# Attention on one core: three score banks and four maxima banks, weighted values in halves, the accumulator out as two tiles, the last pairs with wide exponentials

## The chip, the core and the metric

The kernel runs on one core of a Trainium2 chip. The metric is the time of one execution on the device in microseconds (us). Engines are named as in the profile: PE (TensorE matmul) and PEld (its weight loads), DVE (VectorE), ACT (ScalarE), POOL (GpSimd) and SP (SyncE, which issues most transfers).

## The reference

A block of a transformer for 2048 rows of width 512: softmax attention with 32 heads of width 16, and behind it a gated mixer (gMLP). The change lies in attention and in what takes its output.

```python
h  = x + attention(layernorm(x), wqkv, wo)         # 32 heads, Dh = 16, S = 2048
p  = softmax(q @ k.T / 4)                          # per head, 2048 x 2048
o  = p @ v
h2 = h + mixer(layernorm(h), w_in, w_sp, b_sp, w_out)
```

All is computed in float32 accuracy: q and k as pairs of float16 parts stacked on the contraction rows, the weighted values in float32.

## The kernel before, in words

A first stage projects q, k and v and writes them to memory. Then comes attention, in one loop over 512 units (`hg`, `qb`, `kb`): 8 groups of four heads, 4 query blocks of 512 rows, 16 key blocks of 128 keys. The loop's body handles two units, a **pair**; eight pairs make one query block of a group, here called a block. All engines work in program order, so the order in which the body is written is the order on each engine.

What a pair holds:

- **Scores** (`score`, L778 to 788): eight matmuls `s<-qst,kst`, 128 keys by 512 queries, for two key blocks and four heads. Head index t picks the upper or lower half of the array's rows (rows 0 to 49 or 64 to 113). Each is followed by an exponential on ACT, `pt<-s` (L788). Their PSUM pool `ps_s` has four banks.
- **Maxima steps** (`max_pair`, L205 to 254): the row maxima which softmax subtracts are found eleven pairs ahead (`LEAD`), by eight small steps per pair. A step is a matmul `m<-...,qst` into a bank of `ps_m` (three banks, taken in turn), then a reduction on DVE (`mx<-m`, L228). Two of the steps go together: `minus` takes its bank by an `Abs` on ACT (`ab<-m`, L233), `plus` adds that to its own bank on DVE (L237). The step behind the eighth closes a block's maxima (`nm`, on DVE and POOL), and `max_rows` turns them and writes them into q's spare rows.
- **Weighted values** (`weigh`, L790 to 797): for one key block four float32 matmuls `pv<-pt,vst`, one per head, on four column groups of the array, into one PSUM bank (`ps_v`). Each appears as two records, so one `weigh` is eight records. A ones column in `vst` makes the sum of the exponentials appear as a 17th row of each head. The second key block's `weigh` of a pair is issued in the next pair.

The eighth PSUM bank is `ps_v`'s: 4 + 3 + 1. At a block's end `gather` (L800 to 811) copies the accumulator `pv` to one tile `og`, 256 columns on DVE (L803) and 256 on ACT (L804), and issues eight transfers: values to `o_scr`, sums to a small tile. Three pairs later `invert` takes reciprocals and writes them to `r_scr`.

POOL meanwhile splits and scales the mixer's weights (`work`). The last 11 pairs have no maxima steps. In them the first rows of the output projection start: `load_o` reads o and the reciprocals `rc`, POOL multiplies them (L726), `split_o` makes two float16 parts (L731, L732), `make_h` runs 12 matmuls with `wo` and adds x. Then the mixer's first stage makes all other rows of h in the same manner, one in a step, and later stages follow that the diff does not touch.

The order within a pair before, as the body writes it (s0 to s7 scores, M0 to M7 maxima steps as `max_pair` lists them, W and P the two `weigh`): s0 M0 M1 s1 s2 s3 M2 W M3 M4 s4 s5 s6 M5 turn s7 M6 M7 P, with M3 `minus` and M6 `plus`.

Of the kernel before, what the change touches and what calls it, by code (L numbers as in the profile page):

```python
# [38 lines left out]
VW = DH + 1  # L39
FB = [(i * P, min(P, FH - i * P)) for i in range(6)]  # L40
# [18 lines left out]
def block_kernel(ctx: ExitStack, tc: tile.TileContext, x, wqkv, wo, w_in, w_sp4, b_sp, w_out, out):  # L59
# [25 lines left out]
    o_scr = dram.tile([D, S], F32, name="o_scr")  # L85
# [119 lines left out]
    def max_pair(m):  # L205
# [33 lines left out]
        def last(b):  # L239
            one(1, 3, b)  # L240
# [13 lines left out]
        return [four[0], two[0], two[1], minus, four[1], four[2], plus, last]  # L254
# [15 lines left out]
    with ExitStack() as pre:  # L270
# [260 lines left out]
        todo, done = [], [0]  # L531

        def ahead(k):
            for _ in range(k):
                m = done[0] // 8
                if not todo and m < LEAD:
                    steps = max_pair(m)
                    todo.extend(steps[i] for i in (0, 1, 4, 2, 5, 3, 6, 7))
                if todo:
                    todo.pop(0)(done[0] % 5)  # L540
                    done[0] += 1

# [171 lines left out]
    def load_o(sb):  # L714

        c = slice(sb * P, (sb + 1) * P)
        o = e2.tile([P, DB, P], F32, name="o")
        nc.sync.dma_start(o, o_scr[:, c].rearrange("(d p) s -> p d s", p=P))
        rc = e2.tile([P, DB, P], F32, name="rc")
        for d in range(DB):  # L720
            nc.sync.dma_start(rc[:, d, :], r_scr[8 * d:8 * d + 8, c].rearrange(
                "h (o s) -> h o s", o=1).to_broadcast([8, DH, P]))
# [3 lines left out]
        return lambda: nc.gpsimd.tensor_mul(o, o, rc)  # L726
# [7 lines left out]
    def make_h(sb, acc):  # L734

        o2, h = o2s.pop(sb), xrs[sb]
        for d in range(DB):
            mm3(acc, o2[0][:, d, :], o2[1][:, d, :], wo2[0][:, d, :], wo2[1][:, d, :],
                d == 0, d == DB - 1)
# [17 lines left out]
    def invert():  # L757
# [4 lines left out]
        for j in range(4):  # L762
            nc.sync.dma_start(r_scr[head(hg, j % 2, j // 2), cols].rearrange("(p c) -> p c", c=16),
                              rc[32 * j:32 * j + 32, :])
# [3 lines left out]
    with ExitStack() as at:  # L768
# [9 lines left out]
        def score(hg, qb, kb, p, t):  # L778

            if not t:  # L780
                pts[p, kb] = pp.tile([P, 2, 512], F32, name="pt")
            turn[0] += 1
            pool = later[0] if later and turn[0] % 6 > 3 else ps_s
            s = pool.tile([P, 512], F32, name="s")
            r = slice(RG * t, RG * t + KM)
            nc.tensor.matmul(s, kst[hg % 2][r, p, kb * P:(kb + 1) * P],  # L786
                             qst[hg * NQ + qb][r, p, :], start=True, stop=True)
            nc.scalar.activation(pts[p, kb][:, t, :], s, AF.Exp, scale=scales_[hg // 2])  # L788

        def weigh(hg, qb, kb):  # L790
            if kb == 0:
                pv[0] = ps_v.tile([P, 512], F32, name="pv")
            for j in range(4):
                c = (4 * kb + j) * VW
                nc.tensor.matmul(pv[0][32 * j:32 * j + 32, :], vst[hg % 2][:, c:c + 32],  # L795
                                 pts[j % 2, kb][:, j // 2, :], start=kb == 0, stop=kb == NB - 1)
            for p in range(2):
                del pts[p, kb]

        def gather(hg, qb, pool=sm):  # L800

            o = pool.tile([P, 512], F32, name="og", bufs=2)
            nc.vector.tensor_copy(o[:, :256], pv[0][:, :256])  # L803
            nc.scalar.activation(o[:, 256:], pv[0][:, 256:], AF.Copy)  # L804
            cols = slice(qb * 512, (qb + 1) * 512)
            sums = pool.tile([P, 16], F32, name="sums")
            for j in range(4):
                h = head(hg, j % 2, j // 2)
                nc.sync.dma_start(o_scr[h * DH:(h + 1) * DH, cols], o[32 * j:32 * j + DH, :])
                nc.sync.dma_start(sums[32 * j:32 * j + 32, :], o[32 * j + DH:32 * j + VW, :])  # L810
# [210 lines left out]
        prev, turn, count, later, asked, pts = None, [0], [0], [], [], {}  # L1021
        for n in range(0, len(units), 2):
# [17 lines left out]
            if not steps and not later:  # L1040
                maxima.close()
                later.append(attn.enter_context(
                    tc.tile_pool(name="ps_l", bufs=2, space=PSUM, side="right")))

            def step():
                if steps:
                    steps.pop(0)(count[0] % 3)
                    count[0] += 1

            both = lambda k, p, *ts: [score(hg, qb, k, p, t) for t in ts]  # L1050
            both(kb, 0, 0)
            step()
            step()
            both(kb, 0, 1)
            both(kb, 1, 0, 1)
            step()
            if prev is None:

                pv[0] = ps_v.tile([P, 512], F32, name="pv")
                for j in range(4):  # L1060
                    nc.tensor.matmul(pv[0][32 * j:32 * j + 32, :], vst[0][:, :32],
                                     vst[0][:, :512], start=True, stop=True)
            else:
                weigh(*prev)
            if kb == 0 and n:
                gather(*units[n - 1][:2])
            step()
            step()
            both(kb1, 0, 0, 1)
            both(kb1, 1, 0)  # L1070
            step()
            if turned:
                max_rows()
            both(kb1, 1, 1)
            step()
            step()
            weigh(hg, qb, kb)
# [3 lines left out]
            if n in (486, 490, 506):  # L1081
                asked.append(load_o(h_rows[min((n - 486) // 4, 2)]))
            if n in (492, 496, 508):
                asked.pop(0)()
            if n in (494, 502):
                split_o(h_rows[(n - 494) // 8])
            if n in (500, 504):
                sb = h_rows[(n - 500) // 4]
                make_h(sb, later[0].tile([P, 512], F32, name="h", bufs=1))
# [5 lines left out]
        gather(*prev[:2], e2)  # L1095
# [20 lines left out]
    with ExitStack() as mid:  # L1116
# [67 lines left out]
        with tc.manual_schedule(engines={E.PE, E.Activation, E.DVE, E.Pool, E.SP}):  # L1184
# [3 lines left out]
            for k in range(NB):  # L1188
                sb, new = row[k], row.get(k + 2)
                if new is not None:  # L1190
                    make_h(new, ps.tile([P, 512], F32, name="acc"))
# [207 lines left out]
```

## Time and profile before

| | |
|---|---|
| time, median of 3 runs | 1768.5 us (1768.03 to 1769.24) |
| the profiled execution's own time | 1767.71 us |
| its span, first to last instruction | 1765.9 us |
| attention's pairs with maxima steps | 161.8 to 1275.4 us |
| the last 11 pairs | 1275.4 to 1324.9 us |
| mean granted clock of TensorE | 0.999 |

A row of the timeline gives start, length, engine, line, operation, output and inputs with their shapes, and a count where alike instructions in a row are merged; a bracket holds idle time of the engine ahead of it and what ended that. A row of the groups ends in busy time, mean ns of one, and idle time ahead of them. Since an engine takes up the next instruction before the last one has ended, lengths overlap, and the step from one to the next is shorter than the length of one. Busy time is the union of the lengths.

### The profile page before, as it was taken

How to read it: one execution, taken by the hardware profiler on the slowest of the kernel's cores; microseconds unless marked ns; L12 is line 12 of the kernel's file. 1: busy time of each engine (PE TensorE's matmuls, PEld its weight loads, DVE VectorE, ACT ScalarE, POOL GpSimd, SP SyncE). 2: the span in 40 equal slices, each digit the busy share in tenths (PEclk: the TensorE clock that was granted, in tenths of full speed). 3: DMA queues.
4: the chain of work that ended last, by engine and by line, in shares of the span. 5: the costliest groups of instructions: out<-in, count | busy, mean ns of one | idle time of the engine just before them, and what ended most of it. 6: DMA issues, size and time to landing. Idle time of an engine off the chain costs nothing.

```text
span 1765.9 us, 32751 instructions
## 1 busy us (share of the span) xinstructions
PE 1725.2 (98%) x11621; PEld 643.5 (36%) x11621; DVE 1395.1 (79%) x2896; ACT 1324.2 (75%) x2638; POOL 825.8 (47%) x1088
## 2 busy tenths in 40 slices
PE   9999999999999999999999999999999999999999
PEld 4433222222222222222222222222225666777776
DVE  7688999999999999999999999999825886111112
ACT  4335999999999999999999999999984554011000
POOL 1322677765772178776777667600002765100010
PEclk9999999999999999999999999999999999999999
DMA  5534332242220145335244434300023563753450
GB/s 179 159 101 141 88 84 84 80 91 69 79 58 22 55 122 147 116 115 143 87 147 109 129 113 136 89 16 5 23 64 106 141 178 121 270 186 130 155 182 24
DMA packets 188028, 191.71 MB, mean 109 GB/s; under 512 B 70568, under 2 KB 139240, under 8 KB 187864
## 3 DMA queue, kind: packets, MB, share of 16 engines
q1 hardware_dynamic: 185560, 183.99, 35.6%
q10 hardware_dynamic: 2304, 5.64, 0.8%
q8 instruction: 91, 1.49, 0.4%
q14 instruction: 73, 0.60, 0.1%
HBM read 124.66 MB, written 64.56 MB: 107 GB/s over the span
## 4 chain that ended last, share of the span: by engine, by line
PE 69%; DVE 14%; ACT 11%; DMA 2%; issue 2%; POOL 2%; SPq 1%; DVEq 0%; ACTq 0%; POOLq 0%
PE pv L795 20%; PE m L223 12%; PE s L786 11%; ACT pt L788 7%; DVE mx L228 7%; PE acc L107 4%; PE acc L109 4%; PE acc L108 4%; PE g L107 4%; PE g L108 4%; PE g L109 4%; ACT ab L233 2%; DVE ab L237 1%; DVE rs_t L124 1%; DVE rs_u L126 1%
## 5 line engine op out<-in xcount | busy, mean ns | idle before, releaser
L788 ACT ACTIVATE pt<-s 128x512 f32<-128x512 f32 x2048 | 1042.9, 620 | 7.9 <-PE s L786 5.0
L228 DVE TENSOR_REDUCE mx<-m 128x1 f32<-128x512 f32 x1510 | 963.6, 683 | 21.8 <-PE m L223 3.6
L795 PE MATMUL pv<-pt,vst 128*32 128x512 f32 x4096 | 555.1, 605 | 0.9 <-ACT og L804 0.9
L223 PE MATMUL m<-kst,qst 48*128 48x512 f16 x1510 | 527.6, 379 | 0.1
L786 PE MATMUL s<-qst,kst 50*128 50x512 f16 x2048 | 443.0, 377 | 0.4 <-DVE mx L228 0.4
L223 PEld LDWEIGHTS <-qst 48*128 48x128 f16 x2048 | 143.7, 93 | 389.0 <-issue 376.5
L786 PEld LDWEIGHTS <-kst 50*128 50x128 f16 x2048 | 125.4, 95 | 315.9 <-issue 229.3
L223 PE MATMUL m<-uvs,qst 48*128 48x512 f16 x504 | 190.4, 379 | 24.9 <-ACT ab L233 18.6
L246 POOL TENSOR_SCALAR nm<-nm 128x16 f32<-128x16 f32 x32 | 6.6, 206 | 389.3 <-DVE nm L243 368.8
L237 DVE CUSTOM_DVE_ANT_0 ab<-m,ab 128x512 f32<-128x512 f32 x252 | 171.0, 679 | 7.8 <-PE m L223 5.1
L233 ACT ACTIVATE ab<-m 128x512 f32<-128x512 f32 x252 | 151.8, 602 | 17.1 <-PE m L223 16.4
L795 PEld LDWEIGHTS pv<-pt,vst 128*32 128x32 f32 x4096 | 83.4, 108 | 179.7 <-issue 170.5
L1268 ACT ACTIVATE pT<-tp 128x384 fp32r<-128x384 f32 x32 | 14.0, 488 | 142.1 <-PE tp L1260 142.0
L1346 POOL TENSOR_TENSOR pr<-pr,z 128x344 f32<-128x344 f32 x8 | 7.3, 912 | 193.0 <-DVE pr L1345 181.6
L966 POOL TENSOR_TENSOR op<-raw,op 128x512 f16<-128x512 f32 x80 | 92.8, 1160 | 5.8
L873 POOL TENSOR_TENSOR raw<-raw 128x512 f32<-128x512 f32 (+1 forms) x84 | 83.2, 991 | 6.3
L878 POOL TENSOR_TENSOR acc_sp<-acc_sp,raw 128x512 f32<-128x512 f32 x63 | 80.4, 1277 | 4.4
L107 PE MATMUL acc<-wi,hT 128*128 128x344 f16 x256 | 79.1, 309 | 0.0
L108 PE MATMUL acc<-wi,hT 128*128 128x344 f16 x256 | 79.1, 309 | 0.0
L109 PE MATMUL acc<-wi,hT 128*128 128x344 f16 x256 | 79.1, 309 | 0.0
L1290 DVE TENSOR_TENSOR y<-acc,h 128x512 f32<-128x512 f32 x16 | 11.1, 692 | 85.6 <-PE acc L1286 84.2
L726 POOL TENSOR_TENSOR o<-o,rc 128x512 f32<-128x512 f32 x16 | 20.3, 1270 | 100.1 <-DMA rc<-r_scr 98.3
(233 smaller groups left out, 2297.1 us busy)
## 6 DMA issues: line engine op xcount, KB each, us to landing
raw<-in_w_sp SPq DMA_DIRECT2D x128, 256.0 KB
s_scr<-op SPq DMA_DIRECT2D x64, 256.0 KB
op<-s_scr SPq DMA_DIRECT2D x32, 512.0 KB
a_scr<-op SPq DMA_DIRECT2D x48, 256.0 KB
op<-a_scr SPq DMA_DIRECT2D x24, 512.0 KB
qst<-q_scr SPq DMA_DIRECT2D x192, 32.0 KB
kst<-k_scr SPq DMA_DIRECT2D x48, 128.0 KB
raw<-in_w_in SPq DMA_DIRECT2D x32, 172.0 KB
```

The lines of the kernel that those rows point to most:

```text
L107: nc.tensor.matmul(ps, lh, rh, start=first, stop=False, **kw)
L108: nc.tensor.matmul(ps, lh, rl, start=False, stop=False, **kw)
L109: nc.tensor.matmul(ps, ll, rh, start=False, stop=last, **kw)
L223: nc.tensor.matmul(acc, q[r, p, c], keys[r, p], start=True, stop=True)
L228: nc.vector.reduce_max(at(t, e if t else e - 1), acc, axis=AX.X)
L233: nc.scalar.activation(ab[0], acc, AF.Abs)
L237: nc.vector.tensor_tensor_reduce(ab[0], acc, ab[0], 0.5, LOW, ALU.add, ALU.max, at(0, 0))
L786: nc.tensor.matmul(s, kst[hg % 2][r, p, kb * P:(kb + 1) * P], qst[hg * NQ + qb][r, p, :], start=True, stop=True)
L788: nc.scalar.activation(pts[p, kb][:, t, :], s, AF.Exp, scale=scales_[hg // 2])
L795: nc.tensor.matmul(pv[0][32 * j:32 * j + 32, :], vst[hg % 2][:, c:c + 32], pts[j % 2, kb][:, j // 2, :], start=kb == 0, stop=kb == NB - 1)
L873: pool.tensor_mul(got[0] if n else acc, got[0], got[0])
L966: chores.append((lambda: pool.tensor_sub(t[0][:, 1], of(), t[0][:, 0]), TT))
```

## The change

1. PSUM: `ps_s` has three banks, and a fourth maxima bank `m3` is added, so that steps take four banks in turn.
2. The pair's order is written out in two tables, `PAIR`, and `PAIR0` for the first pair of a block. Scores and maxima steps alternate such that neighbours use different halves of the array's rows. `H` is half of the previous unit's weighted values: 256 of the 512 query columns.
3. The accumulator leaves as two tiles, `og1` (128 columns, ACT) and `og0` (384 columns, DVE), by four transfers into an `o_scr` of 32 rows per head; the sums are read back from there a pair later.
4. In the last 11 pairs two scores share a tile of two banks, and one exponential takes 1024 columns (`scores2`); `make_h` is a generator, whose matmuls come three to a pair.
5. `load_o` reads o by four transfers; `load_o`, its product and `split_o` stand some pairs earlier; `invert` writes by two transfers instead of four.

```diff
+PAIR = "s0 M0 s2 M4 M1 s1 H s3 M2 s5 M3 H M5 s4 M7 s6 turn s7 M6 P".split()
+PAIR0 = "M1 s1 M0 s0 M4 s2 H s3 s4 M5 H out1 M3 out0 s5 M2 M7 s6 turn s7 M6 P".split()
-    o_scr = dram.tile([D, S], F32, name="o_scr")
+    o_scr = dram.tile([DB, 8, 32, S], F32, name="o_scr")
...
-        nc.sync.dma_start(o, o_scr[:, c].rearrange("(d p) s -> p d s", p=P))
+        for d in range(DB):
+            nc.sync.dma_start(o[:, d, :], o_scr[d, :, :DH, c])
...
-        ps_s = at.enter_context(tc.tile_pool(name="ps_s", bufs=4, space=PSUM))
+        ps_m3 = inner.enter_context(tc.tile_pool(name="ps_m3", bufs=1, space=PSUM))
+        ps_s = inner.enter_context(tc.tile_pool(name="ps_s", bufs=3, space=PSUM))
+        more[3] = lambda: ps_m3.tile([P, 512], F32, name="m3")
...
+        def scores2(hg, qb, kb, p):
+            pts[p, kb] = pp.tile([P, 2, 512], F32, name="pt")
+            turn[0] += 1
+            s = later[turn[0] % 3 == 0].tile([P, 2, 512], F32, name="s2")
+            for t in range(2):
+                product(s[:, t, :], hg, qb, kb, p, t)
+            nc.scalar.activation(pts[p, kb], s, AF.Exp, scale=scales_[hg // 2])
-        def weigh(hg, qb, kb):
+        def weigh(hg, qb, kb, a=0, b=512):
...
-                nc.tensor.matmul(pv[0][32 * j:32 * j + 32, :], vst[hg % 2][:, c:c + 32],
-                                 pts[j % 2, kb][:, j // 2, :], start=kb == 0, stop=kb == NB - 1)
+                nc.tensor.matmul(pv[0][32 * j:32 * j + 32, a:b], vst[hg % 2][:, c:c + 32],
+                                 pts[j % 2, kb][:, j // 2, a:b], start=kb == 0, stop=kb == NB - 1,
+                                 skip_group_check=True)
...
-            o = pool.tile([P, 512], F32, name="og", bufs=2)
-            nc.vector.tensor_copy(o[:, :256], pv[0][:, :256])
-            nc.scalar.activation(o[:, 256:], pv[0][:, 256:], AF.Copy)
+            a, b = (0, OG) if i == 0 else (OG, 512)
+            ogs[i] = pool.tile([P, b - a], F32, name=f"og{i}", bufs=2)
+            if i:
+                nc.scalar.activation(ogs[i], pv[0][:, a:b], AF.Copy)
+            else:
+                nc.vector.tensor_copy(ogs[i], pv[0][:, a:b])
...
+            if not steps:
+                scores2(hg, qb, kb, 0)
+                scores2(hg, qb, kb, 1)
+                some_h(2)
+                weigh(*prev)
...
+                scores2(hg, qb, kb1, 0)
+                scores2(hg, qb, kb1, 1)
+                some_h(1)
+                weigh(hg, qb, kb)
...
-            if n in (486, 490, 506):
-                asked.append(load_o(h_rows[min((n - 486) // 4, 2)]))
+            if n in (476, 480, 506):
+                asked.append(load_o(h_rows[min((n - 476) // 4, 2)]))
```

PE's rows before, at the end of an ordinary pair (m0 to m2 are the maxima banks, `uvs` marks the products of `minus` and `plus`, s a score, pv the weighted values):

```order
L223 LDWEIGHTS qst_8807
L223 MATMUL m1_10203<-kst1_1855,qst_8807 128x512
L786 LDWEIGHTS kst1_1855
L786 MATMUL s_10206<-qst_8255,kst1_1855 128x512
L223 LDWEIGHTS qst_8807
L223 MATMUL m2_10209<-uvs1_1856,qst_8807 128x512
L223 LDWEIGHTS qst_8807
L223 MATMUL m0_10212<-kst1_1855,qst_8807 128x512
L795 MATMUL pv_9995<-pt_10158,vst1_163 32x512
L795 MATMUL pv_9995<-pt_10171,vst1_163 32x512
L795 MATMUL pv_9995<-pt_10158,vst1_163 32x512
L795 MATMUL pv_9995<-pt_10171,vst1_163 32x512
```

The `plus` product stands in bank m2, and so did `minus` of this pair, three steps earlier; then comes a whole weighted values. PE's rows now, at the same place:

```order
L226 LDWEIGHTS qst_9788
L226 MATMUL m2_11001<-kst0_164,qst_9788 128x512
L798 LDWEIGHTS kst1_1855
L798 MATMUL s_11005<-qst_9157,kst1_1855 128x512
L798 LDWEIGHTS kst1_1855
L798 MATMUL s_11008<-qst_9157,kst1_1855 128x512
L226 LDWEIGHTS qst_9788
L226 MATMUL m3_11011<-uvs0_165,qst_9788 128x512
L823 MATMUL pv_11014<-pt_10948,vst1_163 32x512
L823 MATMUL pv_11014<-pt_10961,vst1_163 32x512
L823 MATMUL pv_11014<-pt_10948,vst1_163 32x512
L823 MATMUL pv_11014<-pt_10961,vst1_163 32x512
```

`plus` has moved to bank m3, and every maxima product stands beside a score. In the middle of a pair PE now has:

```order
L798 LDWEIGHTS kst1_1855
L798 MATMUL s_10955<-qst_9157,kst1_1855 128x512
L226 LDWEIGHTS qst_9788
L226 MATMUL m2_10958<-kst0_164,qst_9788 128x512
L798 LDWEIGHTS kst1_1855
L798 MATMUL s_10962<-qst_9157,kst1_1855 128x512
L823 MATMUL pv_10403<-pt_10903,vst1_163 32x256
L823 MATMUL pv_10403<-pt_10924,vst1_163 32x256
L823 MATMUL pv_10403<-pt_10903,vst1_163 32x256
L823 MATMUL pv_10403<-pt_10924,vst1_163 32x256
L798 LDWEIGHTS kst1_1855
L798 MATMUL s_10969<-qst_9157,kst1_1855 128x512
```

The weighted values of the previous unit have become two pieces of 256 columns, of which this is the first, with scores and steps between them. DVE's rows at a block's turn before, with what each waits for:

```order
L228 TENSOR_REDUCE mx<-m_12871 128x1 [waits PE_49]
L228 TENSOR_REDUCE mx<-m_12884 128x1 [waits PE_49]
L803 COPY og<-pv 128x256 [waits PE_49]
L228 TENSOR_REDUCE mx<-m_12907 128x1 [waits PE_49]
L228 TENSOR_REDUCE mx<-m_12921 128x1 [waits PE_49]
```

and now:

```order
L231 TENSOR_REDUCE mx<-m_13430 128x1 [waits PE_49]
L231 TENSOR_REDUCE mx<-m_13448 128x1 [waits PE_49]
L837 COPY og_13461<-pv 128x384 [waits DMAHW6_49,DMAHW5_49,Activation_49]
L231 TENSOR_REDUCE mx<-m_13470 128x1 [waits PE_49]
L231 TENSOR_REDUCE mx<-m_13473 128x1 [waits PE_49]
```

The copy of the accumulator has 384 columns in place of 256, and waits for ACT's copy, which stands ahead of it; before, ACT's copy waited for DVE's.

More of the change, by code (lines that the diff above doesn't have):

```diff
@@ L253, in max_pair @@
         two = [lambda b, e=e: one(0, e, b) for e in (2, 3)]
-        return [four[0], two[0], two[1], minus, four[1], four[2], plus, last]
+        return [four[0], two[0], two[1], minus, four[1], four[2], plus, four[3], finish]
     def max_rows():
@@ L538, in ahead @@
                     todo.extend(steps[i] for i in (0, 1, 4, 2, 5, 3, 6, 7))
+                    ends.append(steps[8])
                 if todo:
@@ L737, in make_h @@
         for d in range(DB):
-            mm3(acc, o2[0][:, d, :], o2[1][:, d, :], wo2[0][:, d, :], wo2[1][:, d, :],
-                d == 0, d == DB - 1)
+            for i, (a, b) in enumerate(((0, 0), (0, 1), (1, 0))):
+                nc.tensor.matmul(acc, o2[a][:, d, :], wo2[b][:, d, :],
+                                 start=not (d or i), stop=d == DB - 1 and i == 2)
+                if d < DB - 1 or i < 2:
+                    yield
         nc.vector.scalar_tensor_tensor(h, acc, h_down, h, op0=ALU.mult, op1=ALU.add)
@@ L1041, in block_kernel @@
                 maxima.close()
+                inner.close()
+                later.append(at.enter_context(tc.tile_pool(name="ps_t", bufs=2, space=PSUM)))
                 later.append(attn.enter_context(
[L1043 to L1047, printed above, removed]
-                    count[0] += 1
-            both = lambda k, p, *ts: [score(hg, qb, k, p, t) for t in ts]
@@ L1051, in block_kernel @@
[L1051 to L1077, printed above, removed]
+                    tc.tile_pool(name="ps_l", bufs=1, space=PSUM, side="right")))
+                steps_h.append(make_h(h_rows[0], later[1].tile([P, 512], F32, name="h")))
+            ends = kb == 0 and n
+            def some_h(k):
+                for _ in range(k):
+                    if steps_h and next(steps_h[0], True):
+                        steps_h.pop()
@@ L1190, in block_kernel @@
                 if new is not None:
-                    make_h(new, ps.tile([P, 512], F32, name="acc"))
+                    for _ in make_h(new, ps.tile([P, 512], F32, name="acc")):
+                        pass
                 if k + 1 < NB:
```

106 lines of the change are left out of this document (79 added, 27 removed).

## Prediction

> **What bounds the kernel now.** First the page's shares and slices, then busy time by stage.
>
> ```profile
> PE 1725.2 (98%) x11621; PEld 643.5 (36%) x11621; DVE 1395.1 (79%) x2896; ACT 1324.2 (75%) x2638; POOL 825.8 (47%) x1088
> 161.80:1275.40 1113.60, 1087.55 (x7842) 272.08 (x7838) 1087.05 (x2094) 1105.24 (x2235) 656.29 (x861) 1.00 0.33 90
> 1275.40:1324.90 49.50, 48.62 (x292) 11.08 (x290) 10.09 (x29) 44.89 (x91) 4.39 (x6) 1.00 0.28 70
> ```
>
> The columns of the two stage rows are the stretch, its length, busy time of PE, PEld, DVE, ACT and POOL, granted clock, DMA share and GB/s. The change lives in these two stages: 245 pairs of key blocks that carry maxima steps (1113.6 us), and the last 11 pairs without them (49.5 us). In the first ACT, DVE and PE are all over 97% busy, so a share cannot say who sets the pace. ACT's timeline over one query block of eight pairs (start, length, what) can:
>
> ```profile
> 709.32 0.38 ACT L804 ACTIVATE og<-pv 128x256 f32<-128x256 f32 x1 [0.22 <-DVE og L803]
> 709.60 0.59 ACT L233 ACTIVATE ab<-m 128x512 f32<-128x512 f32 x1
> 714.45 4.08 ACT L788 ACTIVATE pt<-s 128x512 f32<-128x512 f32 x8
> 718.43 0.60 ACT L233 ACTIVATE ab<-m 128x512 f32<-128x512 f32 x1
> 722.90 0.60 ACT L233 ACTIVATE ab<-m 128x512 f32<-128x512 f32 x1
> 745.63 0.39 ACT L804 ACTIVATE og<-pv 128x256 f32<-128x256 f32 x1 [0.22 <-DVE og L803]
> ```
>
> A block takes 745.63 - 709.32 = 36.31 us, an ordinary pair 722.90 - 718.43 = 4.47. ACT has nine 512-column instructions in a pair. What one costs when nothing is missing shows in the last stage:
>
> ```profile
> 1275.46 11.87 ACT L788 ACTIVATE pt<-s 128x512 f32<-128x512 f32 x24 [0.51 <-PE s L786]
> 1286.93 0.98 ACT L731 ACTIVATE o<-o,fig 128x512 f16<-128x512 f32 x1
> 1287.55 2.33 ACT L788 ACTIVATE pt<-s 128x512 f32<-128x512 f32 x4
> 1302.20 4.03 ACT L788 ACTIVATE pt<-s 128x512 f32<-128x512 f32 x8 [2.26 <-PE s L786]
> 1313.00 11.87 ACT L788 ACTIVATE pt<-s 128x512 f32<-128x512 f32 x24 [2.26 <-PE s L786]
> ```
>
> 24 exponentials end within 11.87 us; the first needs 0.60 alone, so each further one ends (11.87 - 0.60)/23 = 0.490 us later. Nine make 4.41, and 72 make 35.28 a block. So ACT is nearly the bound: 0.06 us is lost in an ordinary pair, 36.31 - 35.28 = 1.03 in a block. PE's and ACT's rows of one pair say where the 0.06 goes:
>
> ```profile
> 702.66 0.37 PE L786 MATMUL s<-qst,kst 50*128 50x512 f16 x1
> 702.80 0.38 PE L223 MATMUL m<-kst,qst 48*128 48x512 f16 x1
> 703.11 1.06 PE L795 MATMUL pv<-pt,vst 128*32 128x512 f32 x8
> 704.11 0.39 PE L223 MATMUL m<-uvs,qst 48*128 48x512 f16 x1
> 704.11 0.39 PE L223 MATMUL m<-kst,qst 48*128 48x512 f16 x1
> 704.53 0.60 ACT L233 ACTIVATE ab<-m 128x512 f32<-128x512 f32 x1
> 705.18 0.37 PE L223 MATMUL m<-uvs,qst 48*128 48x512 f16 x1
> 705.31 0.37 PE L223 MATMUL m<-kst,qst 48*128 48x512 f16 x1
> 705.61 0.64 PE L795 MATMUL pv<-pt,vst 128*32 128x512 f32 x4
> ```
>
> The `ab` of the minus product starts when its matmul (704.11 + 0.39) ends, and ends at 705.13; the plus product, three banks later, takes the same bank and starts at 705.18. The weighted values queue behind it until 705.61, the next pair's first score behind those (1.00 later), and ACT behind that score. A loop through one bank, closed twice by whole weighted values of 1.00 us, holds the pair at 4.47.
>
> **The change, ordinary pairs.** Four maxima banks put the plus product on the bank of a reduction that stands two groups of matmuls earlier, so that loop opens. The new order places every score beside a maxima product of the other half of the array's rows; the two that start together at 704.11 show that such a couple runs at once. One step of such matmuls:
>
> ```profile
> 1299.02 0.39 PE L107 MATMUL h<-wo,o 128*128 128x512 f16 x1
> 1301.40 0.38 PE L109 MATMUL h<-wo,o 128*128 128x512 f16 x1
> ```
>
> These are the first and last of 12, (1301.40 - 1299.02)/11 = 0.216. Eight couples take 8 x 0.22 = 1.76. Weighted values cost 704.11 - 703.11 = 1.00, and 0.31 - 0.22 = 0.09 more ahead of them (702.80 to 703.11). No row shows half of one. Nearest are the groups by form:
>
> ```profile
> L795 PE MATMUL pv<-pt,vst 128*32 128x512 f32 x4096 | 555.1, 605 | 0.9 <-ACT og L804 0.9
> L223 PE MATMUL m<-kst,qst 48*128 48x512 f16 x1510 | 527.6, 379 | 0.1
> L107 PE MATMUL acc<-wi,hT 128*128 128x344 f16 x256 | 79.1, 309 | 0.0
> ```
>
> From 379 and 309 ns a column costs 70/168 = 0.417 ns and the rest is 166 ns; so a float32 pass streams 605 - 166 = 439 ns, and two passes 0.88 of the 1.00. Half the columns: 0.44 + 0.12 = 0.56. Bounds: 0.50 (everything halves) and 1.00 (nothing does); I take 0.56, as the rate is that of rows. PE then needs 1.76 + 2 x 0.56 + 1.00 + 3 x 0.09 = 4.15 a pair, under ACT's 4.41.
>
> The Trainium skill, page "TensorEngine Tiling (Array Packing)", section "Key Properties", says that a change of tiling mode drains TensorE, which speaks against a third piece of weighted values. The 0.09 ahead of a piece and the 0.12 in it are that drain in this trace; by the rule the extra piece costs 0.21 a pair, 51 us over 245 pairs, if PE set the pace, and it is in the 4.15 already.
>
> DVE's seven instructions of a pair, by its rows at a block's turn:
>
> ```profile
> 745.18 0.41 DVE L803 COPY og<-pv 128x256 f32<-128x256 f32 x1
> 745.51 1.28 DVE L228 TENSOR_REDUCE mx<-m 128x1 f32<-128x512 f32 x2
> L228 DVE TENSOR_REDUCE mx<-m 128x1 f32<-128x512 f32 x1510 | 963.6, 683 | 21.8 <-PE m L223 3.6
> ```
>
> Two reductions take 1.28, one 0.68, so a step is 0.60 and seven are 4.20: not the bound, but with 0.21 to spare it is late next. Three score banks instead of four: a bank is busy from its matmul (0.38) to the end of its exponential (0.60), 1.1 us with the handovers, and three steps of ACT give 1.47, so none is missed; during 1.09 us of weighted values ACT lives on the scores and the `ab` queued before. I take 4.41 for the pair. It is tight at one place: the exponential behind the first half arrives with no slack, so an error of 0.05 in the half shows. I allow 0.1 a block for it.
>
> **At a block's turn.** ACT's copy falls from 256 columns (709.60 - 709.32 = 0.28) to 128. Columns cost (0.490 - 0.28)/256 = 0.82 ns, so 0.17. DVE's copy grows from 256 to 384: 0.33 (745.18 to 745.51) plus 128 x (0.68 - 0.41)/256 = 0.13, within DVE's spare. The order has ACT's copy first, behind five exponentials, DVE's behind it, and the pair's second weighted values wait for both. From the pair's first exponential: 5 x 0.49 + 0.30 for ACT's copy, + 0.55 for DVE's, + 1.05 for the weighted values, + 0.43 for the next score = 4.8, against 9 x 0.49 + 0.17 = 4.58 of ACT's work: 0.2 to 0.3 lost; I take 0.3. A block is 35.28 + 0.17 + 0.30 + 0.10 = 35.85, which is 0.46 less. 30 blocks are 13.8, the five remaining pairs 5 x 0.06 = 0.3: **-14**. SP issues 6 transfers a block instead of 8, and the sums come back through memory; their reciprocal stands two pairs after that read, so nothing waits.
>
> **The last 11 pairs.** 44 exponentials of 1024 columns replace 88. No row is that wide. Bounds: 2 x 0.490 = 0.98, and 1024 x 0.82 = 0.84; by the slope 0.490 + 512 x 0.82 = 0.91, which I take. They need 44 x 0.91 = 40.0; two copies `o` at 0.62 (1286.93 to 1287.55), 0.2 for og, 0.5 for the change of banks as now: 42.0. The 24 matmuls of two rows of h, which stood in the way as 12 in one piece (twice 2.26 us idle), come three to a pair: PE then has 4 x 0.22 + 3 x 0.22 + 2 x 1.09 = 3.7 a pair, level with ACT's 4 x 0.91. I add 1.0 for that. Now the stage has 49.5 + 0.5: **-7**. The Trainium skill, page "ScalarE: Activation LUTs", section "What ACT_TABLE_LOAD costs", gives 186 ns plus 0.833 ns a column, less 93 ns of overlap; by it, as an estimate, a wide one is 0.946, and the stage 1.6 us longer.
>
> **Behind attention.** One transfer of o per row becomes four, ahead of rc on SP:
>
> ```profile
> 1348.15 1.71 SPq L763 DMA_DIRECT2D r_scr<-rcp  x4
> 1349.96 0.38 SPq L718 DMA_DIRECT2D o<-o_scr  x1
> 1350.38 2.46 SPq L721 DMA_DIRECT2D rc<-r_scr  x4
> 1359.73 1.26 POOL L726 TENSOR_TENSOR o<-o,rc 128x512 f32<-128x512 f32 x1 [13.94 <-DMA rc<-r_scr]
> 1350.00:1375.00 25.00, 22.44 (x132) 13.04 (x130) 15.00 (x50) 11.13 (x19) 13.60 (x16) 0.93 0.51 134
> ```
>
> POOL's wait of 13.94 here reaches PE (2.56 idle of 25, clock 0.93). Three more issues of 0.43 add 1.3, two fewer of r_scr take 0.9 away, once; elsewhere PE's matmuls cover them. Between -1 and +3; I take **+1**.
>
> **Sum.** -14 - 7 + 1 = -20. The profiled execution took 1767.7 (span 1765.9 and 1.8 around it), 0.8 below the median 1768.5. Forecast for the median: 1748.5. 0.2% (3.5 us) is about what this measurement can tell from no change.
>
> **Rivals.**
> *ACT is never late*: no 0.3, no 0.1, wide exponentials at 0.84: 30 x 0.86 = 26, and 10 for the last pairs, 1733 to 1738. Against it stands the chain at the block's turn.
> *The half is dearer*: at 0.66 PE has 4.35 of its own, and the exponentials behind the halves come late by what is added: about 0.06 a pair, the gain of today's loop. The first stage then gives nothing, the last 6, and 1 is lost behind: 1763.5. For it: the tight place; against: a streaming rate of rows.
> *Slower, by the same mechanism further on*: each half keeps most of a whole's price, since it loads its weights and crosses between the two uses of the array again. It decides from 0.67 us a half; at 0.78 PE needs 4.15 + 0.44 = 4.59 a pair, 0.12 over today, +29 in 245 pairs, less 6: 1791; at 1.00 it needs 5.03, +137: 1899. For it: PE is 98% busy now; against: 0.88 of the 1.00 is streaming.
> *It doesn't do what it says*: ACT already ends one per 0.497, so opening the loop only moves the wait to DVE (seven at 0.63 would be 4.41): the first stage -3, the last -4, behind +3: 1764.5, or within 0.2% if the last stage's h matmuls cost ACT their 5 us again.
>
> **How the numbers follow.** Forecast 0.58 (own range 1741 to 1757, from the 0.05 of the half, 0.84 to 0.98 of a wide one and the -1 to +3 behind). Never late 0.12; dearer half 0.13; slower 0.11; not what it says 0.06, of which 0.04 within 0.2%. Faster: 0.58 + 0.12 + 0.13 + 0.02 = 0.85. The range 1736 to 1765 takes the first, half of the second, the third and the last: 0.83.
>
> **What would show it.** Right: the ordinary pair at 4.41 between two `ab`, the block at 35.8 to 35.9, weighted values of 256 columns followed by the next matmul after 0.56, the plus product no longer released by `ab`, DVE's og waiting for ACT's og, no 2.26 us idle in the last stage, wide exponentials ending 0.91 apart. Wrong: halves of 0.67 or more, exponentials released by a score behind a half in every pair, reductions that fall behind, or POOL's 13.94 growing beyond 17.

## The result, and the profile after

The changed kernel takes **1757.7 us** (median of 5 runs, 1755.98 to 1758.66) against 1768.5 before (1766.96 to 1769.24): a ratio of **0.9939**, 95% interval 0.9924 to 0.9953. It is faster by 10.8 us, which lies in the predicted range, and this is about half of the 20 us that were forecast. The profiled execution took 1757.13 us, its span is 1755.4, 10.5 less than before. The three stages of the prediction, cut at the same events as before (first exponential, first exponential without maxima, last exponential, 255.0 us ahead of the end), with the busy time of PE from the page ahead of them:

```profile
PE 1725.9 (98%) x13573; PEld 673.1 (38%) x13573; DVE 1391.0 (79%) x2896; ACT 1310.2 (75%) x2594; POOL 827.5 (47%) x1088
163.97:1264.90 1100.93, 1093.81 (x9794) 304.56 (x9790) 1077.76 (x2092) 1094.92 (x2237) 657.85 (x862) 1.00 0.35 95
1264.90:1308.60 43.70, 42.74 (x288) 8.41 (x286) 10.32 (x29) 42.22 (x47) 2.88 (x5) 1.00 0.18 44
1308.60:1500.40 191.80, 179.44 (x1138) 111.36 (x1138) 132.06 (x407) 88.58 (x155) 105.10 (x124) 0.99 0.47 147
1324.90:1510.90 186.00, 179.33 (x1137) 111.64 (x1134) 128.19 (x407) 89.52 (x155) 103.43 (x123) 0.99 0.50 148
```

(The last row is the kernel before, whose two other stages the prediction shows.) Attention starts 163.97 - 161.80 = 2.2 us later; its first stage is 1113.60 - 1100.93 = 12.7 shorter, its last pairs 49.50 - 43.70 = 5.8; the stretch behind attention is 191.80 - 186.00 = 5.8 longer. 2.2 - 12.7 - 5.8 + 5.8 = -10.5, the whole difference of the spans. So attention gained 18.5 of the 21 forecast, which leaves 2.5 missing there; 2.2 more were lost ahead of it, and 4.8 more than forecast behind it. Behind attention PE's busy time is the same, 179.4 and 179.3: what grew is its idle time, from 6.7 to 12.4 us.

ACT's timeline over a block of the first stage, as it was shown of before:

```profile
705.65 0.30 ACT L835 ACTIVATE og<-pv 128x128 f32<-128x128 f32 x1
705.80 0.63 ACT L236 ACTIVATE ab<-m 128x512 f32<-128x512 f32 x1
719.35 0.62 ACT L236 ACTIVATE ab<-m 128x512 f32<-128x512 f32 x1
723.76 0.62 ACT L236 ACTIVATE ab<-m 128x512 f32<-128x512 f32 x1
741.53 0.30 ACT L835 ACTIVATE og<-pv 128x128 f32<-128x128 f32 x1
```

A block takes 741.53 - 705.65 = 35.88, an ordinary pair 723.76 - 719.35 = 4.41. At the block's turn, and at the first half of weighted values behind it:

```profile
741.86 0.56 DVE L837 COPY og<-pv 128x384 f32<-128x384 f32 x1 [0.32 <-ACT og L835]
742.57 1.06 PE L823 MATMUL pv<-pt,vst 128*32 128x512 f32 x8 [0.29 <-DVE og L837]
744.32 0.64 PE L823 MATMUL pv<-pt,vst 128*32 128x256 f32 x8
744.89 0.39 PE L798 MATMUL s<-qst,kst 50*128 50x512 f16 x1
PE pv L823 <- DVE og L837: 6.0, 27, 0.3
```

DVE's copy waits for ACT's, PE for DVE's. The last row is the whole table of the waits of PE's matmuls between 300 and 1250 us (us in total, times, longest): this 0.3 at each turn is all that they are seen to wait for; the loop through `ab` is gone. Half of the weighted values takes 744.89 - 744.32 = 0.57.

The last pairs on ACT, and PE's groups in a pair that carries h matmuls:

```profile
1264.89 5.87 ACT L816 ACTIVATE pt<-s 128x1024 f32<-128x1024 f32 x6
1270.95 7.75 ACT L816 ACTIVATE pt<-s 128x1024 f32<-128x1024 f32 x8 [0.20 <-PE s L798]
1295.62 12.96 ACT L816 ACTIVATE pt<-s 128x1024 f32<-128x1024 f32 x14
1283.35 0.60 PE L798 MATMUL s<-qst,kst 50*128 50x512 f16 x4
1283.88 0.39 PE L745 MATMUL h<-wo,o 128*128 128x512 f16 x1
1284.20 1.07 PE L823 MATMUL pv<-pt,vst 128*32 128x512 f32 x8
1285.20 0.61 PE L798 MATMUL s<-qst,kst 50*128 50x512 f16 x4
1285.74 0.61 PE L745 MATMUL h<-wo,o 128*128 128x512 f16 x2
1286.27 1.06 PE L823 MATMUL pv<-pt,vst 128*32 128x512 f32 x8
1288.13 1.07 PE L823 MATMUL pv<-pt,vst 128*32 128x512 f32 x8
```

The idle spells of 2.26 us are gone. Such a pair takes 1288.13 - 1284.20 = 3.93 on PE.

Behind attention, SP's transfers for one row, the POOL product that the prediction showed of before, and PE's waits of the stretch (weight loads and matmuls; us in total, times, longest). The last row is the wait of weight loads in the kernel before, 1324.9 to 1510.9:

```profile
1353.02 0.33 SPq L750 DMA_DIRECT2D h_scr<-xr  x1
1353.44 2.47 SPq L724 DMA_DIRECT2D o<-o_scr  x4
1343.17 1.26 POOL L732 TENSOR_TENSOR o<-o,rc 128x512 f32<-128x512 f32 x1 [12.28 <-DMA h_scr<-xr]
PEld L745 <- DVE o L738: 11.6, 10, 2.2
PE acc L745 <- DVE o L738: 6.9, 9, 1.7
PEld L109 <- DVE o L732: 5.0, 7, 1.3
```

The four transfers of o occupy SP for 2.47 us where one took 0.38, and PE's weight loads wait for the DVE part of o's split ten times instead of seven, 11.6 us instead of 5.0.

### The profile page after: what moved, and what is told of

The parts are those of the page before. It is cut to its first block, busy times and chain, and to the rows that moved or that the text cites. A ratio compares the mean times of both kernels' runs of the same rounds, so it can differ in the third digit from the quotient of the medians.

```text
span 1755.4 us, 36700 instructions
## 1 busy us (share of the span) xinstructions
PE 1725.9 (98%) x13573; PEld 673.1 (38%) x13573; DVE 1391.0 (79%) x2896; ACT 1310.2 (75%) x2594; POOL 827.5 (47%) x1088
## 4 chain that ended last, share of the span: by engine, by line
PE 67%; ACT 18%; DVE 6%; DMA 3%; POOL 2%; SPq 2%; issue 2%; ACTq 0%; DVEq 0%; POOLq 0%
PE pv L823 20%; ACT pt L807 15%; PE s L798 13%; PE m L226 7%; PE acc L110 4%; PE acc L112 4%; PE acc L111 4%; PE g L110 4%; PE g L111 4%; PE g L112 4%; ACT ab L236 1%; DMA xr<-in_x 1%; DVE og L837 1%; PE acc L745 1%; DVE mx L231 1%
## 5 line engine op out<-in xcount | busy, mean ns | idle before, releaser
L807 ACT ACTIVATE pt<-s 128x512 f32<-128x512 f32 x1960 | 1006.3, 635 | 10.0 <-PE m L226 6.8
L231 DVE TENSOR_REDUCE mx<-m 128x1 f32<-128x512 f32 x1510 | 938.5, 682 | 15.1 <-PE m L226 5.2
L823 PE MATMUL pv<-pt,vst 128*32 128x256 f32 (+1 forms) x6048 | 599.9, 467 | 6.7 <-DVE og L837 6.5
L798 PE MATMUL s<-qst,kst 50*128 50x512 f16 x2048 | 597.5, 380 | 2.3 <-DVE part L464 1.7
L226 PE MATMUL m<-kst,qst 48*128 48x512 f16 x1510 | 446.5, 382 | 0.0
L798 PEld LDWEIGHTS <-kst 50*128 50x128 f16 x2048 | 132.9, 94 | 331.2 <-issue 301.5
L823 PEld LDWEIGHTS pv<-pt,vst 128*32 128x32 f32 x6048 | 120.0, 108 | 296.6 <-issue 274.3
L226 PEld LDWEIGHTS <-qst 48*128 48x128 f16 x2048 | 153.0, 93 | 207.5 <-issue 157.3
L236 ACT ACTIVATE ab<-m 128x512 f32<-128x512 f32 x252 | 158.3, 628 | 16.5 <-PE m L226 15.8
```

The lines of the kernel that those rows point to most:

```text
L226: nc.tensor.matmul(acc, q[r, p, c], keys[r, p], start=True, stop=True)
L231: nc.vector.reduce_max(at(t, e if t else e - 1), acc, axis=AX.X)
L236: nc.scalar.activation(ab[0], acc, AF.Abs)
L823: nc.tensor.matmul(pv[0][32 * j:32 * j + 32, a:b], vst[hg % 2][:, c:c + 32], pts[j % 2, kb][:, j // 2, a:b], start=kb == 0, stop=kb == NB - 1,
```

## The experiments

Each kernel's time is told as the ratio to the kernel before, measured beside it, with its 95% interval. Where a kernel differs from the one after by a few us, the stages of its profile say more than the two medians.

**1. One part alone: o in four transfers.** The kernel before, with

```diff
-        nc.sync.dma_start(o, o_scr[:, c].rearrange("(d p) s -> p d s", p=P))
+        for d in range(DB):
+            nc.sync.dma_start(o[:, d, :], o_scr[d * P:(d + 1) * P, c])
```

> The kernel before with one part of the change alone: a row of o is loaded by four transfers, one for each 128 channels, instead of one. Theory (SP's issues): each row behind attention puts three further issues of 0.6 us on the chain SP, POOL, ACT, DVE, PE, and the chain is on the path there; the stage behind attention gets 4 to 6.5 us longer, the whole 1773 to 1775 us. Rival (the loss behind attention comes from the new layout of the attended values, or from the smaller remaining lead alone): within 1 us of 1768.5.

Measured: 1775.1 us, 1.0034 (1.0021 to 1.0046). The stretch behind attention and SP's transfers of o for a row:

```profile
1325.50:1519.10 193.60, 181.41 (x1137) 111.73 (x1134) 132.15 (x407) 89.05 (x156) 104.26 (x123) 0.98 0.48 144
1373.01 1.82 SPq L719 DMA_DIRECT2D o<-o_scr  x4
```

It is 193.6 instead of 186.0. 2.1 of the 7.6 is PE's busy time (granted clock 0.98 here); idle time rises from 6.7 to 12.2, close to the 12.4 of the kernel after. This small part of the change, alone, makes the kernel slower, although SP needs only 1.82 - 0.38 = 1.4 us more for a row here. The expected direction is right and its size too small: the stretch grew by 7.6 where 4 to 6.5 were expected.

**2. The same part taken back.** The kernel after, with the attended values laid out so that one transfer does again:

```diff
-    o_scr = dram.tile([DB, 8, 32, S], F32, name="o_scr")
+    o_scr = dram.tile([DB, 32, 8, S], F32, name="o_scr")
...
-        for d in range(DB):
-            nc.sync.dma_start(o[:, d, :], o_scr[d, :, :DH, c])
+        nc.sync.dma_start(o, o_scr[:, :DH, :, c].rearrange("d r h s -> (r h) d s"))
```

(with the rows of `wo` and the reciprocals read in the order row, head, and `o_scr` seen by head where it is written).

> The kernel after, with the attended values laid out so that the 128 rows of a quarter of o stand one behind the other in memory (row within the head ahead of the head), so that one transfer loads all four quarters again; the rows of wo are read in the same order. The outgoing transfers stay two for each part, the sums stay read back. Theory (SP's issues): the lead over the kernel before stays near 17 us through the mixer's first stage, 1751 to 1753. Rival (layout and round trip of the sums, or the lead absorbed anyway): 1757 to 1758, with a loss of about 6 us behind attention still there.

Measured: 1750.2 us, 0.9899 (0.9883 to 0.9914). The stretch behind attention, and SP's transfer of o for a row:

```profile
1307.90:1492.60 184.70, 178.49 (x1138) 111.56 (x1138) 126.82 (x407) 88.67 (x155) 103.63 (x123) 0.99 0.49 150
1363.59 0.39 SPq L723 DMA_DIRECT2D o<-o_scr  x1
```

The stretch is 184.7 instead of 191.8, with 6.2 idle: it is as short as before or shorter, although it starts 17 us earlier than in the kernel before and the sums still go through memory. The whole came out 0.8 under the expected 1751. Experiment 1 has the loss without the new layout, and this run has a layout of 32 rows per head without the loss, so the rivals, layout and absorbed lead, are out.

**3. Four transfers, but ahead of the wait.** The kernel after, with the loads of a row in front of the row's h product:

```diff
                 sb, new = row[k], row.get(k + 2)
+                if k + 4 < NB:
+                    weighted = load_o(row[k + 4])
...
-                        load_o(row[k + 4])()
+                        weighted()
```

> The kernel after, with the loads of a row behind attention (four of o, four of the reciprocals, one of x) issued ahead of the row's h product instead of behind its store to h_scr; the multiplication on POOL stays where it is. Theory (the four issues cost time only because they stand on SP behind a store that waits 6 to 8 us for h, so that o.rc on POOL starts late): with the loads ahead of that wait even four issues are early enough; the loss of 6.4 us behind attention goes, 1749 to 1752. Rival (SP's total of issues, or the transfers themselves, are the limit, wherever they stand): 1756 to 1758.

Measured: 1753.3 us, 0.9913 (0.9899 to 0.9927). The stretch behind attention, ACT's and DVE's part of one split, and the waits of PE's weight loads:

```profile
1308.30:1496.40 188.10, 180.11 (x1138) 112.79 (x1138) 131.27 (x407) 89.54 (x156) 101.26 (x124) 0.98 0.49 149
1381.50 0.72 ACT L737 ACTIVATE o<-o,fig 128x512 f16<-128x512 f32 x1
1385.59 1.42 DVE L738 SCALAR_TENSOR_TENSOR o<-o,fig,o 128x512 f16<-128x512 f32 x1
PEld L745 <- DVE o L738: 8.3, 6, 2.7
```

Idle time falls from 12.4 to 8.0, so most of the loss goes without one transfer fewer: what costs is issues that stand behind the store that waits, not SP's number of issues as such. The time misses the expected 1752 by 1.3, and the rows say where part of the rest is: ACT's part of the split now starts at 1381.50, but DVE's part stands in DVE's order behind the row's scaling (ten small instructions) and starts at 1385.59. PE still waits for DVE's part, 8.3 us in six waits. The Trainium skill, page "DMA: Bandwidth & Descriptors", section "Rules for kernel authors", advises to issue a transfer early and wait for it late. These two traces agree, with 4.4 us less of idle time for the same transfers.

**4. The order of two pools.** The kernel after, with

```diff
-        ps_m3 = inner.enter_context(tc.tile_pool(name="ps_m3", bufs=1, space=PSUM))
         ps_s = inner.enter_context(tc.tile_pool(name="ps_s", bufs=3, space=PSUM))
+        ps_m3 = inner.enter_context(tc.tile_pool(name="ps_m3", bufs=1, space=PSUM))
```

> The kernel after, with two lines in the other order: the pool of score banks is opened ahead of the third maxima bank's. Theory (banks decide the first scores' wait for the last projection): the first exponential starts at 161.8 again instead of 163.97, and the whole is 1.5 to 2.2 us shorter than the kernel after, 1755.5 to 1756.2. Rival (the new order of the first pair, or the accumulator's pool that now comes first, makes the wait): first exponential still near 164, 1757.7.

Measured: 1757.2 us, 0.9935 (0.9921 to 0.9948), which cannot be told from the kernel after. The first score of the kernel after, then ACT's first exponential of the kernel after and of this one:

```profile
163.56 0.37 PE L798 MATMUL s<-qst,kst 50*128 50x512 f16 x1 [1.71 <-DVE part L464]
163.97 1.58 ACT L807 ACTIVATE pt<-s 128x512 f32<-128x512 f32 x3 [4.03 <-PE m L226]
162.02 1.58 ACT L807 ACTIVATE pt<-s 128x512 f32<-128x512 f32 x3 [2.26 <-PE m L226]
```

The cause of the late start is shown: in the kernel after, the first score waits 1.71 for DVE to take the last of the projections' accumulators (`part<-acc`), so its bank was one of theirs; with the pools swapped the start is back at 162.0. The gain does not reach the end: the first stage is 1101.8 long in this run (1100.9 after), and the stretch behind attention 193.2. The expected total, 1755.5 to 1756.2, was wrong.

**5. Weighted values whole again.** The kernel after, with `weigh(*prev)` in one piece at the second `H` and nothing at the first:

```diff
-                    a = 0 if first else 256
-                    weigh(*prev, a, a + 256)
+                    if not first:
+                        weigh(*prev)
```

> The kernel after, with the delayed weighted values of a pair again in one piece of 512 columns, at the place of the second half; three score and four maxima banks and the new order stay. Theory (with three score banks ACT has two exponentials, 0.98 us, ahead of it while PE works on the weighted values, so a whole of 1.06 us starves it and a half of 0.57 does not): about 0.17 us more a pair, a block of 37.2 instead of 35.9, the whole near 1800 us (1785 to 1820). Rival (the halves do nothing but cost PE 0.08 us a pair): 35.9 or less a block, 1755 to 1758.

Measured: 1803.4 us, 1.0194 (1.0180 to 1.0208). A score on PE, and two `ab` on ACT, one pair apart:

```profile
716.32 0.37 PE L798 MATMUL s<-qst,kst 50*128 50x512 f16 x1 [0.25 <-ACT pt L807]
713.43 0.65 ACT L236 ACTIVATE ab<-m 128x512 f32<-128x512 f32 x1
718.07 0.65 ACT L236 ACTIVATE ab<-m 128x512 f32<-128x512 f32 x1
```

The pair is 718.07 - 713.43 = 4.64, 0.23 more than with halves. PE stands 0.25 for a score bank that ACT still reads, 214 times between 300 and 1300 us, and ACT's nine instructions take 4.64. With three score banks ACT keeps its pace over one whole and two halves of weighted values in a pair, and loses it over two wholes. The expected 37.2 a block came out as 764.97 - 727.56 = 37.41 between two of ACT's copies.

**6. Four score banks and three maxima banks with the new order.**

```diff
-        ps_m3 = inner.enter_context(tc.tile_pool(name="ps_m3", bufs=1, space=PSUM))
-        ps_s = inner.enter_context(tc.tile_pool(name="ps_s", bufs=3, space=PSUM))
+        ps_s = inner.enter_context(tc.tile_pool(name="ps_s", bufs=4, space=PSUM))
...
-                    steps[i](count[0] % 4)
+                    steps[i](count[0] % 3)
```

> The kernel after, with the old division of banks: four score banks and three maxima banks; new order, halves and the rest stay. Theory (the new order puts maxima close behind one another, so PE needs a fourth bank to run ahead of DVE at 0.60 us a maximum; without it PE waits for DVE with scores queued behind): 37.5 to 39 us a block instead of 35.88, the whole 1807 to 1855. Rival (the fourth score bank is worth as much to ACT as the fourth maxima bank to DVE): 35.9 a block, 1756 to 1760.

Measured: 1862.0 us, 1.0531 (1.0516 to 1.0546), with a block of 756.29 - 717.00 = 39.29 between two of ACT's copies. Both are slightly beyond what was expected (1855 and 39). Rows of ACT, PE and DVE:

```profile
722.05 0.64 ACT L236 ACTIVATE ab<-m 128x512 f32<-128x512 f32 x1
722.74 0.37 PE L226 MATMUL m<-uvs,qst 48*128 48x512 f16 x1
724.53 2.55 ACT L805 ACTIVATE pt<-s 128x512 f32<-128x512 f32 x5 [0.37 <-PE m L226]
724.50 2.48 DVE L231 TENSOR_REDUCE mx<-m 128x1 f32<-128x512 f32 x4 [0.35 <-PE m L226]
725.85 0.37 PE L226 MATMUL m<-uvs,qst 48*128 48x512 f16 x1
729.42 2.55 ACT L805 ACTIVATE pt<-s 128x512 f32<-128x512 f32 x5 [0.37 <-PE m L226]
```

The plus product starts at 722.74, 0.05 after `ab` has ended at 722.69: with three banks it takes `ab`'s bank again, the loop that the prediction found in the kernel before, and ACT stands 0.37 in every pair of 729.42 - 724.53 = 4.89. The expectation had named another wait, for DVE, and that is there too but smaller: the minus product starts at 725.85, 0.25 behind the score that it stands beside, and 0.07 after DVE's second reduction of the row has ended (724.50 + 0.68 + 0.60 = 725.78). The halves and the fourth maxima bank belong together: with the new order, either of them without the other is slower than the kernel before. The old order with the new banks was not tried.

**7. Narrow exponentials at the end.** The kernel after, with two of 512 columns for each of 1024:

```diff
-            nc.scalar.activation(pts[p, kb], s, AF.Exp, scale=scales_[hg // 2])
+            for t in range(2):
+                nc.scalar.activation(pts[p, kb][:, t, :], s[:, t, :], AF.Exp, scale=scales_[hg // 2])
```

> The kernel after, with each wide exponential of the last 11 pairs as two of 512 columns into the same tiles. Theory (eight of these pairs are bound by PE at 3.93 us because of the three h matmuls, so that only the three pairs without them are bound by ACT): eight exponentials at 0.490 make 3.92 a pair instead of 3.69 in three pairs, 0.5 to 1.5 us more, 1758 to 1759.5. Rival (ACT and PE are both near the bound, so that a dearer ACT is late in every pair): 2.5 to 4 us more, 1760 to 1762.

**8. The h matmuls in lumps.** The kernel after, with `some_h(12)` instead of `some_h(2)`.

> The kernel after, with the 12 matmuls of an h row of the last pairs issued in one go (in the pair where the row begins) instead of three in a pair. Theory (ACT starves while PE works 12 x 0.22 = 2.6 us on one row; the pairs without h matmuls then run at 3.69 instead of 3.93): two pairs with 2.2 us more, less what two filled banks cover, and eight with 0.24 less: 0.5 to 2.5 us more, 1758 to 1760. Rival (the sum of PE's work alone counts): no change, 1757.5.

Measured: 1760.5 us, 0.9954 (0.9940 to 0.9969), and 1760.6 us, 0.9956 (0.9942 to 0.9970); both intervals overlap that of the kernel after, so the stage decides. First the last 11 pairs of the narrow ones and the stretch behind, then the last pairs of the lumps and ACT's idle time at the first of them:

```profile
1264.90:1309.60 44.70, 43.59 (x290) 8.59 (x290) 10.33 (x29) 44.38 (x91) 3.25 (x5) 1.00 0.18 45
1309.60:1506.80 197.20, 181.85 (x1138) 111.87 (x1135) 133.34 (x407) 88.40 (x155) 104.46 (x123) 0.98 0.45 142
1264.80:1311.60 46.80, 45.16 (x288) 10.26 (x286) 10.07 (x29) 41.38 (x46) 4.52 (x5) 1.00 0.20 52
1269.33 11.11 ACT L816 ACTIVATE pt<-s 128x1024 f32<-128x1024 f32 x12 [2.65 <-PE s L798]
```

Narrow exponentials cost 44.7 - 43.7 = 1.0 us in their stage, as expected. The median lies 2.8 above the kernel after, outside the expected total and in the rival's. But the profiled execution (1763.5 us, the longest of five) has the rest behind attention (197.2 instead of 191.8, at a clock of 0.98), where no narrow one runs; in the kernels with four transfers behind the wait that stretch differs by some us (191.4 to 197.2 in the runs of this study). Lumps cost 46.8 - 43.7 = 3.1, more than the expected 0.5 to 2.5, with an idle spell of 2.65 in ACT. So of what the last pairs gained the spreading is the larger part.

**9. Both cures together, and two further steps.** One transfer and swapped pools (the first), the loads ahead of the wait as well (the second), and h matmuls two in a pair instead of three (the third, without the early loads):

> Both edits together: one transfer for a row of o, and the score banks' pool ahead of the third maxima bank's. Theory (with one transfer the rows behind attention no longer take back a lead, so that what attention gains by the earlier start stays): 1.1 us less than the kernel with one transfer alone (the end of the exponentials moved by 1.1 in the run with the pools swapped), 1748.5 to 1749.8. Rival (what is gained earlier is always absorbed behind attention): 1750 to 1751.

> The same, with the loads of a row also issued ahead of its h product. Theory (with the early loads DVE's part of the split becomes the late one, 20.9 us for two rows instead of 20.05): the rows run as in the run with early loads alone, 3 us more behind attention than with one transfer alone, 1751 to 1753. Rival (SP's issues were the only limit and the two cures add): 1745 to 1749.

> One transfer and swapped pools, with the h matmuls of the last pairs spread as two in a pair (three in the last two pairs) instead of three in eight pairs; the second row's split, its h bank and the two scalings move back by two or three pairs for it. Theory (eight pairs are bound by PE at 3.93 us; with two matmuls they come to 3.28 + 2 x 0.22 = 3.72): the last 11 pairs 1 to 1.7 us shorter, 0.5 to 1.7 us less than both edits alone. Rival (ACT's 3.69 and the later h of the second row take it back): no change, or up to 1 us more.

Measured: 1749.5 us, 0.9891 (0.9875 to 0.9908); **1745.8 us, 0.9866 (0.9849 to 0.9882)**; 1752.5 us, 0.9905 (0.9888 to 0.9921). The stretch behind attention of the first and second, and the last pairs and that stretch of the third:

```profile
1307.00:1490.50 183.50, 178.34 (x1138) 112.04 (x1138) 126.95 (x407) 88.77 (x155) 104.04 (x123) 0.99 0.49 152
1307.40:1492.00 184.60, 177.06 (x1138) 111.10 (x1138) 130.92 (x407) 87.93 (x155) 102.18 (x123) 1.00 0.46 150
1263.40:1305.80 42.40, 41.55 (x288) 8.22 (x286) 7.67 (x19) 41.97 (x47) 4.54 (x6) 1.00 0.26 51
1305.80:1495.30 189.50, 179.99 (x1138) 112.15 (x1138) 131.24 (x418) 88.51 (x155) 101.46 (x122) 0.98 0.48 147
```

The first cannot be told from one transfer alone (0.9899), though its last exponential is 0.9 us earlier. The second came out faster than its theory, in the range of its rival (1745 to 1749). The stretches do not show why: the profiled execution of the second is the longest of its four (1748.83), that of the first the shortest (1747.26), and the second has 7.5 us idle against 5.2 in the first. Whether the early loads gain anything on top of the first is open; the intervals of the two overlap. The second has the lowest median of all, about 12 us under the kernel after. The third shortens the last pairs by 1.3, as expected, and loses 6.0 behind them against the first, with 9.5 us idle. So its rival was right that the gain is taken back, but the median is 2.9 above the first where the rival allowed up to 1. The likely cause is that the second row of h is complete three pairs later; that was not tried by itself.

## Why the prediction was right, and where its sum was off

Measured by the spans the kernel gained 10.5 where 20 were forecast. The missing 9.5 is 1.3 in the first stage, 1.2 in the last pairs, 2.2 at the start of attention and 4.8 behind it.

- **Ordinary pair, 4.41: right.** Measured 4.41. The half, which no row of before showed, was taken at 0.56 and measured 0.57; the four maxima banks opened the loop, and experiment 6 closes it again.
- **Block, 35.85: right.** Measured 35.88. Of that 35.28 is ACT's work and 705.80 - 705.65 = 0.15 its copy, which leaves 0.45 lost where 0.40 was taken. The chain named, ACT's copy, DVE's copy, PE, is in the rows with waits of 0.32 and 0.29. The stage gave 12.7 of the 14. From the first copy to the 30th (202.97 to 1244.15, before 200.71 to 1254.35) 29 blocks gained 0.43 each where 0.46 was taken, and the first block gained nothing (39.00 from the first exponential to the copy, 38.91 before). Against eight ordinary pairs the turn cost 36.31 - 8 x 4.47 = 0.55 before and costs 35.88 - 8 x 4.41 = 0.60 now: the gain is in the pairs and the turn shows none. The new way out of the accumulator was not tried by itself.
- **Start of attention: a term that was missing.** 2.2 us. The diff shows the order of the pools; I read it for the number of banks and not for which banks they are. 1.71 of it is the first score's wait.
- **Last pairs, -7: the step that failed is PE's 3.7 a pair.** Wide exponentials end (12.96 - 1.02)/13 = 0.92 apart in the 14 from 1295.62 on, behind the last h matmul (the first of them takes 1.02), where 0.91 was taken. But PE needs 3.93 in a pair with h matmuls: four scores take 1283.88 - 1283.35 = 0.53 (two couples at 0.22 and 0.09 for the crossing that I had counted), one h matmul 1284.20 - 1283.88 = 0.32, two 0.53. Each group of h matmuls is 0.1 dearer than its steps, since it stands between scores and weighted values and adds a second crossing there; I had counted one. The sum is 2 x (0.53 + 1.00) + 0.32 + 0.53 = 3.91. ACT's four wide exponentials are 4 x 0.92 = 3.68, so eight such pairs lose 8 x 0.25 = 2.0, where I added 1.0. The Trainium skill, page "TensorEngine Tiling (Array Packing)", section "Key Properties", says that a change of tiling mode drains TensorE. That rule bears on these groups too, and these rows put 0.1 us to it. The Trainium skill, page "ScalarE: Activation LUTs", section "What ACT_TABLE_LOAD costs", gave 0.946 as an estimate for a wide exponential. The trace has 0.92.
- **Behind attention, +1: the largest error, +5.8.** Two steps failed. An issue was taken at 0.43 and took 2.47/4 = 0.62, so a row costs SP 2.1 more, not 1.3. And I set a cost of one row, less a saving that comes once, as if PE's matmuls covered the other rows. They don't: SP stands behind the h store until h is there, and the row's transfers, POOL's product and the split follow in a chain, so that PE's weight loads wait ten times for the split. The sign that I had named for it, POOL's wait growing beyond 17 us, did not appear (the same product waits 12.28 after), and it is no sign: in experiment 2, which loses nothing, a product behind attention waits 19.13 (at 1329.51). The sign that counts is PE's wait for the split. Experiments 1, 2 and 3 show it from three sides.
- **The rivals.** ACT is late at every block's turn, so "never late" did not happen; a half of 0.57 leaves out the dearer half and the slower case; and the change does what it says. (The slower case has a slip: by its own prices PE passes ACT's 4.41 at a half of 0.69, 4.15 + 2 x 0.13, not at 0.67.) Experiment 5 shows how near the slow side lies: the same order with one whole in place of the two halves is 2% slower than before.

The result falls between the forecast and the second rival's 1763.5, but not for that rival's reason. The forecast's own range (1741 to 1757) misses it by 0.7. That the wider range holds it is partly luck: it reached up to 1765 for rivals that did not come true, and the late start of attention stood in none of the sums.

## What to carry to other kernels

When an edit adds a DMA issue, look for the wait ahead of it on its queue: four transfers instead of one, 2.1 us more of issues in a row, raised PE's idle time over the stretch from 6.2 (experiment 2) to 12.4 us where they stand behind a store that waits, and to 8.0 where they stand ahead of it. Where two engines share PSUM through small rings of banks, settle the order, the size of the pieces and the division of banks together; with the new order, leaving out the halves or the fourth maxima bank made this kernel 2 or 5% slower than before. And read a change of pools for the banks that each gets as well as for their number: here the first user of a bank waited 1.71 us for the last user of the stage before.

## What the runs showed of the hardware

SP's time for a transfer follows its address pattern more than its bytes: in most rows 256 KB of o in one transfer take 0.39 us, 64 KB of rows that stand one behind the other 1.82/4 = 0.46, the same 64 KB as 8 groups of 16 rows 2.47/4 = 0.62. A group of h matmuls, which use the full array, set between scores and weighted values, which use parts of it, costs 0.1 us once beside 0.22 for each matmul (0.32 for one, 0.53 for two), since four scores take 0.53 with it or without (1297.52 - 1296.98 = 0.54 to the weighted values of a pair that has none). The wide exponential (1024 columns over two banks) takes 0.92 against 2 x 0.49, which was worth 1.0 us in this kernel.
